# Expert stage of a fused mLSTM and two-layer MoE kernel: two output scalings of the first expert moved behind its third block, weight splits regrouped, one scaling of the last expert moved

## The chip, the cores and the metric

One NeuronCore of one Trainium2 chip runs the whole program in one launch. The metric is the device time of the program in microseconds (us), as a median of several executions. The engines are named as the profile names them: PE (TensorE), DVE (VectorE), ACT (ScalarE), POOL (GpSimd) and SP (SyncE, which here only issues DMAs).

## The reference, cut to what matters

Three layers follow one another. The change lies in the third alone.

```python
x = mlstm(q, k, v, gates)                 # (1536 tokens, 320)
x = leaky(x @ w_in) @ w_out               # dense layer, 320 -> 2048 -> 320
e = argmax(x @ w_gate, axis=1)            # each token goes to one of 8 experts
disp[e, slot] = x[token]                  # capacity 384 slots per expert
h = max(disp @ w1[e], 0)                  # 320 -> 1024
y = h @ w2[e]                             # 1024 -> 320
out[token] = gate_w[token] * y[e, slot]   # 0 where a token found no slot
```

## The kernel before, in words

**Layout of the expert stage** (lines 838 to 967). The routed rows lie in a DRAM buffer `scr`, 384 slots for each expert. An expert's slots are three blocks of 128, `j` = 0, 1, 2. For each block there are four steps:

- `hidden(e, j)` (L586 through `l1_chunk`): 8 chunks of 128 hidden units, each of 8 matmuls (values are kept as a high and a low float16 part), 64 matmuls in all, into two PSUM banks `h`, one for each half `u` of the chunks.
- `evict(e, j)`: for each half, ACT writes the high part `hh` with a ReLU (L888) and DVE the low part `hl` (L889).
- `outs(e, j)` (L590 to L592 through `l2_chunk`): 8 chunks of 3 matmuls, 24 in all, into the PSUM tile `py`. The first two of a chunk read `hh`, the third (L592) reads `hl`.
- `deliver(e, j)`: ACT scales `py` by the tokens' gate weight into `ye` (L900), and POOL issues an indirect DMA that scatters the rows of `ye` to the output (L901). The gate weights and token numbers come in one small load `mt` (L850).

**Blocks that are not there.** Block 0 is always computed. `if_block(e, j)` is a branch on PE alone: where expert `e` has no tokens in block `j`, PE jumps over `hidden` and `outs` of it. ACT and DVE still run their evictions and scalings for such a block. With these inputs 15 of the 24 blocks hold tokens: the experts 0 to 7 have 1, 2, 3, 2, 1, 1, 3 and 2 of them.

**Weights.** An expert's two matrices come in two pieces, so there are 16 pieces, 0 to 15; expert `e` uses 2e and 2e+1. A piece has an "in" part (from `w1`: a staging tile `wa`, loaded by L542 and L543) and an "out" part (from `w2`: a staging tile `wc`, loaded by L552). Each part must be split into a high and a low float16 half before PE may use it: ACT writes the high half (L498) and DVE the low half (L499). The in split is two instructions on each engine (128x1024 and 64x512), the out split one on each (128x1280). There are four staging tiles of each kind, and a load is issued when the split that last read its tile is done; SP issues loads in order.

**Order of the work.** The whole expert stage stands in `manual_schedule`: PE, ACT and DVE run their instructions in the order in which the code gives them. POOL's and SP's order is set by the framework's planner. The splits are laid in between the steps by hand: while expert `e` is computed, the pieces of `SPLITS[e]` are split, which are [4], [5, 6, 7], [8, 9, 10], [11, 12, 13], [14], [15], and none for the last two (L32). The list `bg` holds an in and an out split for each piece (and in expert 0 the out splits of the pieces 2 and 3 ahead of those of piece 4). `some(k)` (L926) runs the `k`-th quarter of `bg`, rounded down. The order within one expert on ACT and DVE is this: evict block 0, `some(0)`, deliver block 2 of the expert before, evict block 1, `some(1)`, deliver block 0, `some(2)`, deliver block 1, evict block 2, `some(3)`. PE's order is: hidden block 0, outs block 2 of the expert before, hidden block 1, outs block 0, outs block 1, hidden block 2. In the last expert there is no next one, so its blocks are closed on the spot (L958 to L967).

Of the kernel before, what the change touches and what calls it, by code (L numbers as in the profile page):

```python
# [75 lines left out]
def tile_mlstm_moe_moe(  # L76
# [191 lines left out]
    def run_all(fs):  # L268
        for f in fs:
            f()  # L270
# [259 lines left out]
    def w_place(n):  # L530
        staged[n, 2] = pool_of.get(n, wpb).tile([P, PCN], F16, tag="pc", name=f"pc{n}")
# [40 lines left out]
    def w_out_split(n):  # L572
        c = staged[n, 1]
        if n < NP1:
            rc, c = c, stage_out()
            narrow(c, rc)
        pieces[n][1] = piece_out(pieces[n][1], c, src_of(n)[3], n in PPOOL)
# [10 lines left out]
    def l2_chunk(py, n, kc, gh, gl, first, last):  # L588
        oh, ol = pieces[n][1]
        nc.tensor.matmul(py, lhsT=gh, rhs=oh[:, kc, :], start=first, stop=False)  # L590
        nc.tensor.matmul(py, lhsT=gh, rhs=ol[:, kc, :], start=False, stop=False)  # L591
        nc.tensor.matmul(py, lhsT=gl, rhs=oh[:, kc, :], start=False, stop=last)  # L592
# [87 lines left out]
    def apart(key, dma):  # L680

        tc.declare_no_dep(dma.ins, group=key, reason="each token has a row of its own")
        tc.add_to_no_dep_group(key, dma.ins)
# [139 lines left out]
    def w_load(n):  # L823
        w_alloc(n)
        w_load_in(n)
        w_load_out(n)
# [16 lines left out]
    def exp_load(e):  # L843
        X[e] = e2.tile([P, 6, NSLOT], F16, tag=f"xe{e % 2}", name=f"xe{e}")
        nc.sync.dma_start_transpose(out=X[e], in_=scr[e * NSLOT:(e + 1) * NSLOT, 0:384].bitcast(F16))

    def meta_load():

        mt = e2.tile([P, E, NJ, 2], F32, name="mt")
        nc.sync.dma_start(mt, scr[:, 384:386].rearrange("(e j p) c -> p e j c", p=P, j=NJ))  # L850
        ix = e2.tile([P, E, NJ], I32, name="ix")
        nc.gpsimd.tensor_scalar(out=ix, in0=mt[:, :, :, 0], scalar1=IDX0, scalar2=None, op0=ALU.add)
        T["meta"] = mt, ix
# [19 lines left out]
    def wn(e, c):  # L873
        return NP1 + e * NP2 + c // NKC, c % NKC
# [17 lines left out]
    def outs(e, j):  # L892
        hh, hl = hhl[e % 2]
        for c in range(NCK):
            l2_chunk(py[j], *wn(e, c), hh[:, c, j * P:(j + 1) * P], hl[:, c, j * P:(j + 1) * P], c == 0, c == NCK - 1)

    def deliver(e, j):
        mt, ix = (x[:, e] for x in T["meta"])
        ye = yes[e % 2]
        nc.scalar.activation(ye[:, j], py[j], AF.Copy, scale=mt[:, j, 1:2])  # L900
        apart("out", nc.gpsimd.indirect_dma_start(  # L901
            out=out, out_offset=bass.IndirectOffsetOnAxis(ix[:, j:j + 1], 0), in_=ye[:, j],
            in_offset=None, bounds_check=NT - 1, oob_is_err=False))
# [6 lines left out]
    for e in range(E):  # L910
        if e + 1 < E:
            exp_load(e + 1)
        if e == 0:
            meta_load()
        bg = [lambda: w_out_split(NP1 + 2), lambda: w_out_split(NP1 + 3)] if e == 0 else []
        for n in SPLITS[e]:
            n += NP1
            if (n, 0) not in staged:
                w_load(n)
            w_place(n)  # L920
            bg += [lambda n=n: w_in_split(n), lambda n=n: w_out_split(n)]
        for n in sum(SPLITS[e + 1:], [])[0:NLOAD]:
            if (NP1 + n, 0) not in staged:
                w_load(NP1 + n)

        def some(k, of=4):  # L926
            run_all(bg[k * len(bg) // of:(k + 1) * len(bg) // of])

        hidden(e, 0)
        if e == 0:  # L930
            for t in hs[NU:] + py[1:]:
                nc.vector.memset(t, 0.0)
        evict(e, 0)
        some(0)
        if e == 0:
            _, more = nc.values_load_multi_w_load_instructions(
                filled[0:1].rearrange("a e j -> a (e j)"), engines=[ENG.PE], min_val=0, max_val=1,
                skip_runtime_bounds_check_because="it is the outcome of a comparison")
        else:
            with if_block(e - 1, 2):  # L940
                outs(e - 1, 2)
            deliver(e - 1, 2)
        with if_block(e, 1):  # L943
            hidden(e, 1)
        evict(e, 1)
        some(1)
        outs(e, 0)
        deliver(e, 0)
        some(2)
        if e < E - 1:  # L950
            with if_block(e, 1):
                outs(e, 1)
                with if_block(e, 2):
                    hidden(e, 2)
            deliver(e, 1)
            evict(e, 2)
            some(3)
        else:  # L958
            with if_block(e, 2):
                hidden(e, 2)  # L960
            evict(e, 2)
            with if_block(e, 2):
                outs(e, 2)
            deliver(e, 2)
            with if_block(e, 1):
                outs(e, 1)
            deliver(e, 1)  # L967
    one.close()

# [28 lines left out]
```

## Time and profile before

| | us |
|---|---|
| median of three runs | 424.47 |
| the three runs | 424.04, 424.47, 424.86 |
| the profiled execution, whole | 424.7 |
| its span, first to last instruction | 423.0 |

The profiled execution is 0.23 us above the median of the runs, inside their spread of 0.82 us; its span leaves out 1.7 us that lie around it. All times of rows below count from the start of that span. The expert stage begins at 299.6 us and runs to the end, so it is 123 us of the 423.

How to read the rows: a row of a timeline gives start, length, engine, line, operation, what it writes and reads, and how many neighbouring instructions were merged; in square brackets stands how long the engine was idle just before, and what ended the idle time as the profile infers it. "PEq" is PE's sequencer (branches, semaphores), "PEld" its weight loads. The granted clock of PE is given as a share: 1.00 is 2.4 GHz, 0.50 is 1.2 GHz.

### The profile page before, as it was taken

The page shows a single profiled execution, that of the slowest core. Times are in us where ns is not written, and L with a number is a line of the kernel's source. Part 1 is how long each engine was busy: PE and PEld are TensorE (multiplying, and loading weights), DVE is VectorE, ACT ScalarE, POOL GpSimd, SP SyncE. Part 2 cuts the span into 40 slices and gives each one's busy share as a digit, 9 for nine tenths or more (in the row PEclk, how much of TensorE's full clock was granted, in tenths as well). Part 3 has the DMA queues.
Part 4 walks back from the last instruction along what each step waited for, and adds up shares of the span by engine and source line. Part 5 has one row for each costly group of instructions (what it writes and reads, how often), then busy time and mean ns, then how long its engine had stood idle before and what let it go on. Part 6 is the DMA issues. An engine that isn't in the chain of part 4 may idle for free. (4 is left out here: it accounts for less than half of the span.)

```text
span 423.0 us, 9186 instructions
## 1 busy us (share of the span) xinstructions
PE 367.9 (87%) x3597; PEld 286.3 (68%) x3597; DVE 300.8 (71%) x516; ACT 227.6 (54%) x440; POOL 170.8 (40%) x207
## 2 busy tenths in 40 slices
PE   0878657889799998999999999798779999789993
PEld 0767547668588875666656666595667898568882
DVE  8998999998669664877563374756689967866121
ACT  4461647427676747555355354751378966765222
POOL 4451651816446562465734373443124212222102
PEclk9999999669989999999999999999899999899999
DMA  9999999757998866099611349996197989722000
GB/s 172 218 296 233 262 246 211 126 108 154 210 191 122 176 153 135 2 240 180 152 43 32 60 158 302 303 238 195 45 218 218 312 223 347 169 63 61 33 17 19
DMA packets 146130, 70.22 MB, mean 166 GB/s; under 512 B 115666, under 2 KB 136692, under 8 KB 146080
## 3 DMA queue, kind: packets, MB, share of 16 engines
q1 hardware_dynamic: 144160, 65.44, 67.2%
q0 software_dynamic: 1920, 4.08, 2.7%
q8 instruction: 35, 0.57, 0.6%
q14 instruction: 15, 0.12, 0.1%
HBM read 43.65 MB, written 13.17 MB: 134 GB/s over the span
## 5 line engine op out<-in xcount | busy, mean ns | idle before, releaser
L586 PEld LDWEIGHTS <-pc 128*128 128x128 f16 x1728 | 117.9, 101 | 34.0 <-issue 11.5
L586 PE MATMUL h<-xT,pc 128*128 128x128 f16 (+3 forms) x768 | 99.6, 282 | 5.0 <-DMA xT<-xr 3.0
L801 POOL TENSOR_TENSOR gl<-t,gh 128x512 f16<-128x512 f32 (+1 forms) x52 | 60.0, 1155 | 63.6 <-ACT gh L800 63.4
L586 PE MATMUL h<-xe,pc 128*128 128x128 f16 x960 | 57.3, 222 | 5.5 <-PEq L940 2.0
L590 PE MATMUL px<-pc,gh 128*128 128x320 f16 x192 | 58.2, 305 | 2.1 <-ACT gh L800 2.1
L901 POOL DMA_INDIRECT out_dram<-ye,ix x24 | 26.7, 1114 | 81.1 <-ACT ye L900 80.1
L591 PE MATMUL px<-pc,gh 128*128 128x320 f16 x192 | 58.2, 305 | 0.0
L592 PE MATMUL px<-pc,gl 128*128 128x320 f16 x192 | 56.3, 306 | 0.6 <-POOL gl L801 0.6
L799 DVE SCALAR_TENSOR_TENSOR t<-h,t 128x512 f32<-128x512 f32 (+1 forms) x52 | 33.4, 644 | 30.0 <-ACT t L798 29.8
L889 DVE SCALAR_TENSOR_TENSOR hl<-h,hh 128x512 f16<-128x512 f32 x48 | 31.3, 685 | 32.4 <-ACT hh L888 32.3
L800 ACT ACTIVATE gh<-t 128x512 f16<-128x512 f32 (+1 forms) x52 | 30.9, 594 | 29.1 <-DVE t L799 28.6
L798 ACT ACTIVATE t<-h 128x512 f32<-128x512 f32 (+1 forms) x52 | 28.9, 555 | 29.5 <-PE h L586 28.9
L499 DVE SCALAR_TENSOR_TENSOR pc<-wa,pc 128x1024 f16<-128x1024 f32 (+1 forms) x36 | 36.9, 1024 | 8.9 <-ACT pc L498 6.8
L590 PE MATMUL py<-pc,hh 128*128 128x320 f16 x120 | 36.6, 305 | 3.1 <-PEq L943 2.3
L888 ACT ACTIVATE hh<-h 128x512 f16<-128x512 f32 x48 | 27.1, 594 | 21.5 <-PE h L586 20.2
L592 PE MATMUL py<-pc,hl 128*128 128x320 f16 x120 | 36.7, 306 | 1.6 <-DVE hl L889 1.5
L498 ACT ACTIVATE pc<-wa 128x1024 f16<-128x1024 f32 (+1 forms) x36 | 29.6, 863 | 15.3 <-DVE wa L483 9.0
L591 PE MATMUL py<-pc,hh 128*128 128x320 f16 x120 | 36.6, 305 | 0.0
L499 DVE SCALAR_TENSOR_TENSOR pc<-wc,pc 128x1280 f16<-128x1280 f32 x20 | 31.4, 1571 | 3.7 <-ACT pc L498 3.5
L498 ACT ACTIVATE pc<-wc 128x1280 f16<-128x1280 f32 x20 | 25.3, 1266 | 2.3 <-DVE wc L483 2.2
L590 PEld LDWEIGHTS <-gh 128*128 128x128 f16 x192 | 19.2, 100 | 10.8 <-ACT gh L800 2.6
L900 ACT ACTIVATE ye<-py,mt 128x320 f32<-128x320 f32 x24 | 12.4, 525 | 26.0 <-PE py L592 11.9
(178 smaller groups left out, 658.5 us busy)
## 6 DMA issues: line engine op xcount, KB each, us to landing
wc<-in_moe_w_dram SPq DMA_DIRECT2D x16, 640.0 KB, 6.5
wa<-in_moe_w_dram SPq DMA_DIRECT2D x16, 512.0 KB, 9.8
raw<-in_moe_w_out_dram SPq DMA_DIRECT2D x4, 1280.0 KB
scr<-zero SPq DMA_DIRECT2D x8, 588.0 KB, 4.4
raw<-in_moe_w_in_dram SPq DMA_DIRECT2D x4, 1024.0 KB
lb<-lam_d SPq DMA_DIRECT2D x8, 512.0 KB, 4.6
wa<-in_moe_w_dram SPq DMA_DIRECT2D x16, 128.0 KB
qkv<-in_k_dram SPq DMA_DIRECT2D x12, 160.0 KB, 2.9
```

The source lines that it names most:

```text
L498: nc.scalar.activation(hi, x, AF.Copy, scale=s)
L499: nc.vector.scalar_tensor_tensor(out=lo, in0=x, scalar=s, in1=hi, op0=ALU.mult, op1=ALU.subtract)
L586: nc.tensor.matmul(ph, lhsT=w, rhs=xT[:, x, 0:ncol], start=(m == 0), stop=(m == len(seq) - 1))
L590: nc.tensor.matmul(py, lhsT=gh, rhs=oh[:, kc, :], start=first, stop=False)
L591: nc.tensor.matmul(py, lhsT=gh, rhs=ol[:, kc, :], start=False, stop=False)
L592: nc.tensor.matmul(py, lhsT=gl, rhs=oh[:, kc, :], start=False, stop=last)
L798: nc.scalar.activation(t, ph, AF.Copy, scale=0.01 * S_G)
L799: nc.vector.scalar_tensor_tensor(out=t, in0=ph, scalar=S_G, in1=t, op0=ALU.mult, op1=ALU.max)
L800: mark[0] = nc.scalar.activation(gh, t, AF.Copy)
L801: nc.gpsimd.tensor_tensor(out=gl, in0=t, in1=gh, op=ALU.subtract)
L888: nc.scalar.activation(hh[:, to[0], to[1]], ph, AF.Relu)
L889: nc.vector.scalar_tensor_tensor(out=hl[:, to[0], to[1]], in0=ph, scalar=0.0, in1=hh[:, to[0], to[1]], op0=ALU.max, op1=ALU.subtract)
```

## The change

Three things, all in the loop over the experts, none of which touches what is computed.

1. `some(k)` rounds its bounds up where it rounded down. In expert 0 (four splits) nothing changes, one in each group. In experts 1 to 3 (six splits) the groups were 1, 2, 1, 2 and become 2, 1, 2, 1. In experts 4 and 5 (two splits) they were 0, 1, 0, 1 and become 1, 0, 1, 0.
2. In expert 0 the two `deliver` calls of the blocks 0 and 1 move behind the eviction of block 2 and the last group of splits.
3. In the last expert `deliver` of block 2 is given after `outs` of block 1, directly ahead of `deliver` of block 1.

```diff
         def some(k, of=4):
-            run_all(bg[k * len(bg) // of:(k + 1) * len(bg) // of])
+            run_all(bg[-(-k * len(bg) // of):-(-(k + 1) * len(bg) // of)])
...
         outs(e, 0)
-        deliver(e, 0)
+        if e > 0:
+            deliver(e, 0)
         some(2)
         if e < E - 1:
             with if_block(e, 1):
                 outs(e, 1)
                 with if_block(e, 2):
                     hidden(e, 2)
-            deliver(e, 1)
+            if e > 0:
+                deliver(e, 1)
             evict(e, 2)
             some(3)
+            if e == 0:
+
+                deliver(e, 0)
+                deliver(e, 1)
         else:
             with if_block(e, 2):
                 hidden(e, 2)
             evict(e, 2)
             with if_block(e, 2):
                 outs(e, 2)
-            deliver(e, 2)
             with if_block(e, 1):
                 outs(e, 1)
+            deliver(e, 2)
             deliver(e, 1)
```

## Rows read from the trace of the kernel before

**Rows 1.** Page, part 1: busy time of PE over the span.
```profile
PE 367.9 (87%) x3597; PEld 286.3 (68%) x3597; DVE 300.8 (71%) x516; ACT 227.6 (54%) x440; POOL 170.8 (40%) x207
```

**Rows 2.** Waits of PE, 299 to 423 us: total, times, longest.
```profile
PE py L592 <- DVE hl L889: 1.5, 1, 1.5
```

**Rows 3.** Timeline of PE in expert 4, `outs` of its only block.
```profile
365.78 0.30 PE L590 MATMUL py<-pc,hh 128*128 128x320 f16 x1 [0.57 <-PEq L943]
...
367.73 0.45 PE L592 MATMUL py<-pc,hl 128*128 128x320 f16 x1 [1.51 <-DVE hl L889]
...
371.16 0.30 PE L590 MATMUL py<-pc,hh 128*128 128x320 f16 x1
...
372.25 0.30 PE L592 MATMUL py<-pc,hl 128*128 128x320 f16 x1
```

**Rows 4.** Windows: length, busy (PE PEld DVE ACT POOL), PEclk, DMA share, GB/s.
```profile
365.78:367.73 1.95, 0.43 (x3) 0.11 (x3) 1.95 (x3) 1.95 (x5) 0.85 (x1) 1.00 0.98 303
367.73:371.14 3.41, 3.41 (x13) 1.94 (x14) 3.38 (x5) 1.30 (x2) 0.19 (x1) 0.50 0.05 12
371.14:372.60 1.46, 1.41 (x10) 0.78 (x8) 0.17 (x1) 0.00 (x0) 0.00 (x0) 1.00 0.00 0
```

**Rows 5.** Timeline of ACT, end of expert 3 and start of expert 4.
```profile
358.29 1.26 ACT L498 ACTIVATE pc<-wc 128x1280 f16<-128x1280 f32 x1
361.13 0.53 ACT L900 ACTIVATE ye<-py,mt 128x320 f32<-128x320 f32 x1 [1.57 <-issue]
361.55 1.07 ACT L888 ACTIVATE hh<-h 128x512 f16<-128x512 f32 x2
362.50 1.57 ACT L498 ACTIVATE pc<-wa 128x1024 f16<-128x1024 f32 x2
363.97 1.26 ACT L498 ACTIVATE pc<-wc 128x1280 f16<-128x1280 f32 x1
365.13 1.06 ACT L888 ACTIVATE hh<-h 128x512 f16<-128x512 f32 x2
```

**Rows 6.** Timeline of DVE in the same stretch.
```profile
359.72 1.49 DVE L499 SCALAR_TENSOR_TENSOR pc<-wc,pc 128x1280 f16<-128x1280 f32 x1
...
363.61 1.94 DVE L499 SCALAR_TENSOR_TENSOR pc<-wa,pc 128x1024 f16<-128x1024 f32 x2
365.58 1.49 DVE L499 SCALAR_TENSOR_TENSOR pc<-wc,pc 128x1280 f16<-128x1280 f32 x1
366.99 2.48 DVE L889 SCALAR_TENSOR_TENSOR hl<-h,hh 128x512 f16<-128x512 f32 x4
```

**Rows 7.** Timelines of ACT, DVE, PE and PEld, experts 0 and 1.
```profile
311.08 0.53 ACT L900 ACTIVATE ye<-py,mt 128x320 f32<-128x320 f32 x1 [2.29 <-DMA mt<-scr]
...
312.58 1.94 DVE L499 SCALAR_TENSOR_TENSOR pc<-wa,pc 128x1024 f16<-128x1024 f32 x2 [1.80 <-ACT pc L498]
314.56 1.29 DVE L889 SCALAR_TENSOR_TENSOR hl<-h,hh 128x512 f16<-128x512 f32 x2
...
315.51 3.58 PEld L586 LDWEIGHTS <-pc 128*128 128x128 f16 x64 [1.42 <-DVE hl L889]
315.52 3.74 PE L586 MATMUL h<-xe,pc 128*128 128x128 f16 x64 [1.25 <-PEq L940]
```

**Rows 8.** Timeline of PE's weight loads in expert 5, first `hl` of `outs`.
```profile
377.89 0.10 PEld L592 LDWEIGHTS <-hl 128*128 128x128 f16 x1 [0.39 <-DVE hl L889]
```

**Rows 9.** Line L951, PE's branch over an absent block 1: min/median/max ns, first, last.
```profile
L951 PEldq COMPARE_BRANCH  x7: 63/68/3846, 306.5 to 390.1; - x7
```

**Rows 10.** Timeline of POOL: two scatters one right behind the other.
```profile
374.72 0.98 POOL L901 DMA_INDIRECT out_dram<-ye,ix  x1 [0.30 <-ACT hh L888]
```

**Rows 11.** Timeline of SP, expert 3: load of piece 13, next `xe` load.
```profile
347.16 0.46 SPq L542 DMA_DIRECT2D wa<-in_moe_w_dram  x1
...
361.16 2.52 SPq L845 DMA_TRANSPOSE xe<-scr  x1
```

**Rows 12.** Line L542: time from issue of a `wa` load to its landing.
```profile
DMA to landing us min/median/max: 6.4/9.8/10.3
```

## The prediction

> **What bounds the kernel now.** I read the page first: PE is busy 87% of the span [rows 1], so a change in the expert stage is worth what it takes out of PE's own waits there. The second view was PE's waits from 299 us to the end. Most are branch costs of PE's sequencer, which no order on ACT or DVE touches. One is not: a single wait of 1.5 us for DVE's `hl` [rows 2]. The third view, PE's timeline, places it. In expert 4 `outs` starts at 365.78, and its third matmul, the first that reads `hl`, starts only at 367.73 [rows 3]. The fourth view, the windows, shows a second loss right behind. In the 3.41 us that follow, PE's granted clock is 0.50, the lower level of 1.2 GHz, in a stretch where PE never stops; in the 1.95 us before it PE was busy for 0.43 [rows 4].
>
> What both cost: the matmuls from 367.73 to 371.16 are 13 steps in 3.43 us, 0.264 each; those from 371.16 to 372.25 are 8 steps in 1.09 us, 0.136 each [rows 3]. Low clock: 13 x (0.264 - 0.136) = 1.66 us. Wait: without it the third matmul starts two steps after 365.78, at 366.05, so 1.68 us. The sum, 3.34 us, checks against the whole: `outs` of 24 matmuls lasts from 365.78 to 372.55, 6.77 us, where 23 steps of 0.136 and a last one of 0.30 make 3.43.
>
> Why DVE is late there: ACT and DVE run in order. ACT is released from the scaling of expert 3's block 1 at 361.13, evicts its absent block 2 (361.55), then splits both parts of piece 13 (362.50, 363.97), and only then evicts expert 4's block 0 (365.13) [rows 5]. DVE repeats that order: in split 363.61, out split 365.58, then `hl` of expert 4 from 366.99 [rows 6]; its first half ends about 367.7. In front of 361.13 ACT was idle for 1.57 us [rows 5]. That slot is what the regrouping can use.
>
> **The change part by part.**
>
> *Regrouping, experts 1 to 3.* The groups become 2, 1, 2, 1. In expert 3 the in split of piece 13 moves ahead of the scaling at 361.13, into the idle slot. On ACT the step from 362.50 to 363.97 shows that it takes 1.47 us; behind the out split of piece 12 (358.29, 1.16 to the next instruction by the step 363.97 to 365.13) it runs from 359.45 to 360.92, so the scaling still starts at 361.13 [rows 5]. ACT then evicts block 2 at 361.55 as now, the out split starts at 362.50 and expert 4's eviction at 363.66 instead of 365.13. DVE: the out split of piece 12 waits for ACT as now or a little less; I place it at 359.6, ending a step of 1.41 later (365.58 to 366.99) at 361.0. The in split follows for 1.97 (363.61 to 365.58) to 362.97, the two `hl` of block 2 for some 1.2 (half of the 2.48 for four) to 364.18, the out split to 365.59, and then the first `hl` of expert 4, 0.69 long, to 366.28 [rows 6]. PE wants it at 366.05, so 0.25 us of the wait is left. Ends: no wait is left, or all 1.51 (the rival "as before" below); I take 0.25 because every step of it is a row from the same stretch.
>
> With the wait down to 0.25 us PE has no stretch like the one that precedes the low clock [rows 4], so I let the 1.66 us go as well; that they stay is a rival. Gain: 3.34 - 0.25 = 3.09 us.
>
> By the Trainium skill, "TensorE: Matmul & The Clock Gate", section "Why this matters for your kernels", only a longer idle gap than this one of 1.51 us brings the clock down. By that rule the low stretch has another cause and stays, and only 1.43 us are gained; the trace, whose clock falls at the end of this wait, speaks against it.
>
> The other side of 2, 1, 2, 1: one more out split, 1.41 us of DVE [rows 6], now stands ahead of the eviction of block 1 in experts 1, 2 and 3. What waits behind it is `outs` of block 1. PE first runs `outs` of block 0, 24 x 0.136 = 3.3 us [rows 3], so this is covered wherever DVE is level with PE. It is least so in expert 1, where DVE works off what expert 0 left; there the second part helps, since DVE's idle 1.80 us at 312.58 [rows 7] exceeds the 1.41. If that cover were gone, PE would wait there for at most the 1.41 us. I cost it at nothing. Staging tiles come free no later than now, so no load on SP starts later, except that the planner may set SP's order anew (a rival).
>
> *Regrouping, experts 4 and 5.* The out split of piece 14 now stands ahead of the scaling of block 1 and the eviction of block 2, the in split ahead of the older scaling. The work in front of expert 5's eviction is the same. `outs` of expert 5 shows a small wait now: 0.39 us in the weight loads [rows 8], less one step of 0.136 about 0.25 on PE. DVE no longer waits for ACT in that stretch. Ends 0 and 0.25 gained; I take 0.15.
>
> *Expert 0.* ACT waits 2.29 us for `mt` in front of the scaling at 311.08, and DVE 1.80 in consequence [rows 7]. Behind it stand the split of piece 4, the eviction of block 2 and then expert 1's first eviction. After the change ACT does all of that meanwhile; the two scalings and their two scatters come when `mt` is there, with nothing behind them on POOL until the next scaling. The loads that wait for piece 4's staging tiles are issued up to 1.8 us sooner. Does PE gain? The profile says that the weight loads at 315.51 waited for `hl`, whose first half ends at 315.25, and that PE stood 1.25 us, ended by its sequencer at L940 [rows 7]. Taken at its word, about 0.9 us would go (1.25 less a branch cost of some 0.3). But the same hidden block comes right after the dearest branch of all, 3.85 us at L951 [rows 9], and PE's own stream may be what was late. The ends are 0.9 gained and, as the same bound the other way (weight loads now run beside that stream sooner), 0.9 lost. I take nothing, since PE's releaser is the sequencer and the `hl` row only coincides.
>
> By the Trainium skill, "Runtime: NRT & Kernel Launch", section "Instruction fetch mechanics", a taken branch out of the loaded pages waits for a fetch by DMA; the 3.85 us agree. That would put the 1.25 us on the fetch and give this part no gain, which is the 0 above; by the releaser alone the sum would be 0.9 lower.
>
> *Last expert.* ACT's order stays: scaling of block 2, then of block 1. If its wait is still for its own block, nothing changes. If it is now for the `outs` in front of it, both scalings come at the end, and the second scatter is issued one POOL step later, 0.98 + 0.30 = 1.28 us [rows 10]. Ends 0 and +1.28; I take 0.
>
> **Sum.** 3.09 + 0.15 = 3.24 us less. The profiled execution of 424.7 would become 421.5; its 0.23 us above the median are within the runs' spread, so from 424.47 I forecast **421.2 us**.
>
> **The rivals.**
>
> - *The low clock stays*: what is gained is the wait, 1.68 - 0.25 = 1.43, and 0.15, so 422.9 us. For it: the wait is short, and PE had a branch pause of 0.57 us in front of it as well, which stays [rows 3]. Against: the low stretch begins at 367.73, just where the wait ends [rows 3, 4].
> - *Expert 0 pays too*: 0.9 more, 420.3 us. For it: the releaser in the weight loads. Against: PE's own row names the sequencer.
> - *The last scaling waits for the last `outs`*: 421.2 + 1.28 = 422.5 us. The change in the last expert then does something; otherwise it does nothing.
> - *As before*: the wait in expert 4 keeps its 1.51 us, since DVE, not ACT, sets it and has as much to do; with the low clock behind it the time is 424.3 us. Against: between the end of its out split at 361.21 and the in split at 363.61 DVE has 2.40 us with only the 1.21 of two `hl` in it, so 1.2 us of idle time lie ahead of the critical `hl` and get filled [rows 6].
> - *Slower*: the in split of piece 13 now stands in front of the scaling at 361.13, so ACT stands if its load is not there. With a split start S, the first `hl` of expert 4 ends at S + 1.1 + 1.97 + 1.21 + 1.41 + 0.69 = S + 6.4, against 367.7 now: it decides from S = 361.3 on. The load is issued at 347.16 [rows 11] and the slowest of its line takes 10.3 us [rows 12], 357.5, so there is 3.8 us to spare. Only another order on SP undoes that: behind the next `xe` load (361.16 + 2.52) it would land at 374.0 and `hl` would end at 380.4, 12.7 us later than now, 437 us.
>
> **How the numbers follow.** Chances: forecast 0.66 (its own range 420.6 to 421.9), low clock stays 0.12, expert 0 pays too 0.08, last scaling waits 0.05, as before 0.04, slower 0.05. A measurement of this kernel can tell about 0.2%, 0.85 us, from no change. The first four are faster by more than that; since "as before" could fall either way and waits can turn up that no row shows, I put faster 0.88, same 0.06, slower 0.06. The range 420.1 to 423.0 holds the forecast, the rivals at 420.3, 422.5 and 422.9, and the 0.9 lost in expert 0; outside lie as before and slower, and the tails.
>
> **What would show each step.** Right: ACT's in split of piece 13 directly behind the out split of piece 12, no 1.57 us of idle time there; expert 4's eviction about 1.5 us sooner after the scaling; the wait of `outs` in expert 4 for `hl` at 0.3 us or less; PE's clock at 1.00 through experts 4 and 5; ACT without a wait for `mt` in front of piece 4. Wrong: a 0.50 stretch that remains, a new wait of `outs` on block 1 in expert 1, an ACT wait on a `wa` load, or the last two scatters back to back.

## The result and the profile after

The changed kernel takes 419.71 us (median of 7 runs, 418.33 to 420.72) where the kernel before, on the same chip, takes 424.04 (7 runs, 421.99 to 424.86): a ratio of 0.9907, 95% interval 0.988 to 0.9933. It is faster, as forecast, but by about 4 us and not 3.24: the time lies 0.4 us below the forecast range. The profiled execution of after took 420.25 us, its span is 418.5.

One profiled execution against one other says little about tenths of a microsecond here, so the comparison below uses several. Five profiles have the instruction order of before on PE, ACT, DVE and SP (before itself and the runs `last_only`, `control_look`, `scatter_late` and `gate_before`, told below), three that of after (after, `after_again`, `after_gate`). Each stretch runs from the start of PE's first matmul of a block to that of the next one named, read from PE's timeline.

| stretch of PE's timeline, us | before | order of before, mean of 5 | after | order of after, mean of 3 | difference of means | forecast |
|---|---|---|---|---|---|---|
| expert 0 to expert 1 | 10.95 | 10.55 | 10.28 | 10.66 | +0.11 | 0 |
| expert 1 to expert 4 | 50.93 | 51.48 | 50.00 | 50.02 | -1.46 | 0 |
| expert 4 to expert 5 | 11.23 | 10.58 | 8.42 | 8.22 | -2.36 | -3.09 |
| expert 5 to expert 6's third block | 23.07 | 23.02 | 22.37 | 22.70 | -0.32 | -0.15 |
| from there to PE's end | 21.57 | 21.57 | 21.57 | 21.57 | 0 | 0 |
| sum | 117.75 | 117.20 | 112.64 | 113.17 | -4.03 | -3.24 |

The -4.03 of the means agrees with the timed difference of 4.3. The part in expert 4 is a little smaller than forecast, and a part between experts 1 and 4 was forecast as nothing.

The page of after, part 1, shows PE's share of the span unchanged at 87%, and 5.6 us less of PE's busy time than in [rows 1] for the same 3597 matmuls. Of these, 3.1 us lie in the expert stage, where before has the lower clock at two places and after at none until its end; the other 2.5 us lie ahead of it, where the change touches nothing, and are a difference between two executions.

```profile
PE 362.3 (87%) x3597; PEld 283.1 (68%) x3597; DVE 296.2 (71%) x516; ACT 227.7 (54%) x440; POOL 177.0 (42%) x207
```

In PE's waits of after from 299 to 419 us (total, times, longest), the 1.5 us of [rows 2] are gone. What is left for `hl` is 0.56 us in the first `outs` of expert 0 and 0.17 in expert 5. The branch costs of PE's sequencer lead the list, as they did before:

```profile
PE py L590 <- PEq L943: 3.0, 3, 1.4
...
PE py L592 <- DVE hl L889: 0.7, 2, 0.6
```

PE's timeline of after in expert 4 answers to [rows 3]. The third matmul follows the second after 0.14 us, where it came 1.8 later before; the last of the 24 starts at 368.40:

```profile
365.28 0.30 PE L590 MATMUL py<-pc,hh 128*128 128x320 f16 x1 [1.01 <-PEq L943]
365.41 0.30 PE L591 MATMUL py<-pc,hh 128*128 128x320 f16 x1
365.55 0.30 PE L592 MATMUL py<-pc,hl 128*128 128x320 f16 x1
...
368.40 0.30 PE L592 MATMUL py<-pc,hl 128*128 128x320 f16 x1
```

The windows of after over the same 24 matmuls (length, busy PE, PEld, DVE, ACT, POOL, granted clock, DMA share, GB/s) show the upper clock throughout, against 0.50 in [rows 4]:

```profile
365.28:368.71 3.43, 3.42 (x24) 2.24 (x24) 3.37 (x6) 2.45 (x5) 0.98 (x1) 1.00 0.41 90
```

ACT's and DVE's timelines of after at the end of expert 3 answer to [rows 5, 6]. The in split of piece 13 (358.50) stands directly behind the out split of piece 12, the 1.57 us of idle time in front of the scaling (now at 360.18) are gone, and expert 4's first eviction starts 2.54 us after that scaling, before 4.00. DVE has the first `hl` of expert 4 done halfway through its 1.28 us from 364.62, before PE asks for it at 365.55:

```profile
357.34 1.26 ACT L498 ACTIVATE pc<-wc 128x1280 f16<-128x1280 f32 x1
358.50 1.56 ACT L498 ACTIVATE pc<-wa 128x1024 f16<-128x1024 f32 x2
360.18 0.53 ACT L900 ACTIVATE ye<-py,mt 128x320 f32<-128x320 f32 x1
360.60 1.07 ACT L888 ACTIVATE hh<-h 128x512 f16<-128x512 f32 x2
361.56 1.28 ACT L498 ACTIVATE pc<-wc 128x1280 f16<-128x1280 f32 x1
362.72 0.61 ACT L888 ACTIVATE hh<-h 128x512 f16<-128x512 f32 x1
...
360.05 1.93 DVE L499 SCALAR_TENSOR_TENSOR pc<-wa,pc 128x1024 f16<-128x1024 f32 x2
362.01 1.29 DVE L889 SCALAR_TENSOR_TENSOR hl<-h,hh 128x512 f16<-128x512 f32 x2
363.22 1.48 DVE L499 SCALAR_TENSOR_TENSOR pc<-wc,pc 128x1280 f16<-128x1280 f32 x1
364.62 1.28 DVE L889 SCALAR_TENSOR_TENSOR hl<-h,hh 128x512 f16<-128x512 f32 x2
```

ACT's and PE's timelines of after in experts 0 and 1 answer to [rows 7]. ACT splits piece 4 and evicts block 2 first, and still waits 1.26 us for `mt`, but now nothing that PE needs soon stands behind it. PE's pause between expert 1's two hidden blocks is 0.32 us, before 1.25:

```profile
307.89 1.57 ACT L498 ACTIVATE pc<-wa 128x1024 f16<-128x1024 f32 x2
309.82 1.08 ACT L888 ACTIVATE hh<-h 128x512 f16<-128x512 f32 x2 [0.36 <-PEq L952]
310.79 1.27 ACT L498 ACTIVATE pc<-wc 128x1280 f16<-128x1280 f32 x1
313.33 0.94 ACT L900 ACTIVATE ye<-py,mt 128x320 f32<-128x320 f32 x2 [1.26 <-DMA mt<-scr]
...
310.52 3.73 PE L586 MATMUL h<-xe,pc 128*128 128x128 f16 x64 [0.83 <-DMA xe<-scr]
314.57 1.62 PE L586 MATMUL h<-xe,pc 128*128 128x128 f16 x26 [0.32 <-PEq L940]
```

### The profile page after: what moved, and what is told of

Same layout as the page of the kernel before. It is cut to its first block, busy times and chain, and to the rows that moved or that the text cites. A ratio compares the mean times of both kernels' runs of the same rounds, so it can differ in the third digit from the quotient of the medians.

```text
span 418.5 us, 9184 instructions
## 1 busy us (share of the span) xinstructions
PE 362.3 (87%) x3597; PEld 283.1 (68%) x3597; DVE 296.2 (71%) x516; ACT 227.7 (54%) x440; POOL 177.0 (42%) x207
## 4 chain that ended last, share of the span: by engine, by line
PE 37%; issue 22%; POOL 12%; DMA 11%; DVE 10%; ACT 4%; SPq 2%; POOLq 1%; DVEq 0%; ACTq 0%
PE h L586 15%; POOL out_dram L901 6%; PE px L592 4%; PE px L590 4%; PE px L591 4%; DMA raw<-in_moe_w_in_dram 3%; POOL gl L801 3%; DMA lb<-lam_d 2%; DMA wc<-in_moe_w_dram 2%; PE pj L408 2%; PE pj L407 2%; ACT lb L321 1%; DVE pc L499 1%; PE pi L395 1%; DMA x2T<-x2r 1%
## 5 line engine op out<-in xcount | busy, mean ns | idle before, releaser
L801 POOL TENSOR_TENSOR gl<-t,gh 128x512 f16<-128x512 f32 (+1 forms) x52 | 65.3, 1257 | 63.2 <-ACT gh L800 63.0
L901 POOL DMA_INDIRECT out_dram<-ye,ix x24 | 30.0, 1251 | 71.0 <-ACT ye L900 70.4
L586 PE MATMUL h<-xe,pc 128*128 128x128 f16 x960 | 55.9, 219 | 3.6 <-PEq L940 1.0
L590 PE MATMUL py<-pc,hh 128*128 128x320 f16 x120 | 35.9, 299 | 3.8 <-PEq L943 3.0
L499 DVE SCALAR_TENSOR_TENSOR pc<-wc,pc 128x1280 f16<-128x1280 f32 x20 | 29.7, 1486 | 9.3 <-ACT pc L498 9.1
L591 PE MATMUL py<-pc,hh 128*128 128x320 f16 x120 | 35.9, 299 | 0.0
L592 PEld LDWEIGHTS <-gl 128*128 128x128 f16 x192 | 18.9, 99 | 13.1 <-POOL gl L801 5.7
```

What stands on the lines that cost most here:

```text
L499: nc.vector.scalar_tensor_tensor(out=lo, in0=x, scalar=s, in1=hi, op0=ALU.mult, op1=ALU.subtract)
L586: nc.tensor.matmul(ph, lhsT=w, rhs=xT[:, x, 0:ncol], start=(m == 0), stop=(m == len(seq) - 1))
L801: nc.gpsimd.tensor_tensor(out=gl, in0=t, in1=gh, op=ALU.subtract)
L901: apart("out", nc.gpsimd.indirect_dma_start(out=out, out_offset=bass.IndirectOffsetOnAxis(ix[:, j:j + 1], 0), in_=ye[:, j], in_offset=None ...
```

## The experiments

Ratios are to runs of the kernel before on the same chip in the same session, with 95% intervals. The letters in the first four quoted expectations belong to those texts; from the fifth run on, A is "ACT's wait for `mt` makes `hl` late, and PE waits", and C is "POOL's first scatter, issued just ahead of PE's branch L940, delays PE there".

### The three parts alone, and the wait filled

**The regrouping alone** (`regroup_only`):

```diff
-            run_all(bg[k * len(bg) // of:(k + 1) * len(bg) // of])
+            run_all(bg[-(-k * len(bg) // of):-(-(k + 1) * len(bg) // of)])
```

> The weight splits in groups of 2, 1, 2, 1 alone; expert 0 and the last expert as before. Theory A (the forecast's working): nearly all of the gain is here. The third matmul of outs in expert 4 waits 0.3 us or less where it waited 1.68, and the clock stays at 1.00 behind it: 3.1 to 3.3 us less than before, ratio about 0.9925. Theory B (expert 0's part pays as well, about 0.9 us in the first hidden block of expert 1): this part gives the same 3.1 to 3.3 us, and the hidden block of expert 1 still takes 4.7 us from start to release. Theory C (the two parts only pay together, since DVE's backlog of expert 0 now runs into outs of block 1 in expert 1): a new wait of about 0.2 to 1.4 us of PE for hl in expert 1, and a gain of 2 us or less.

Measured: 422.86 us, ratio 0.9944 (0.9917 to 0.997), some 2.4 us and not 3.1 to 3.3. In its profile expert 4's `outs` lasts 3.69 us, at the upper clock, with 0.27 us of the wait left, the size that the prediction put down.

**Expert 0's part alone** (`first_only`), all else as before:

```diff
-        deliver(e, 0)
+        if e > 0:
+            deliver(e, 0)
...
-            deliver(e, 1)
+            if e > 0:
+                deliver(e, 1)
             evict(e, 2)
             some(3)
+            if e == 0:
+                deliver(e, 0)
+                deliver(e, 1)
```

> Expert 0's two scalings behind its third block, nothing else. Theory A: ratio 1.000 within 0.2%; ACT no longer waits for mt ahead of piece 4, but the first hidden block of expert 1 ends when it did and the 1.68 us wait and the low clock in expert 4 stay. Theory B: about 0.95 us less, ratio about 0.9978, with the first hidden block of expert 1 taking 3.75 us instead of 4.7 from start to release, and all later steps shifted by the same amount.

Measured: 423.03 us, ratio 0.9942 (0.9913 to 0.997), again some 2.4 us, more than either theory expected. The part that was costed at nothing gives as much as the one that was costed at 3.24, within the intervals. In its profile expert 4 is as before (`outs` 6.79 us, low clock), and the stretch from expert 1 to expert 4 is 50.00 us, as in after.

**The last expert's part alone** (`last_only`):

```diff
-            deliver(e, 2)
             with if_block(e, 1):
                 outs(e, 1)
+            deliver(e, 2)
             deliver(e, 1)
```

> The last expert's scaling of block 2 given after outs of block 1, nothing else. All theories: ratio 1.000 within 0.2%, since ACT's order is the same; the scaling of block 2 still starts some 2.7 us before that of block 1. The rival of the forecast (the scaling waits for the last outs): both scalings back to back at the end, 1.28 us more, ratio 1.003. If the first hidden block of expert 1 takes 3.75 us here too, its 4.7 us of before are no property of the order but differ from one execution to the next.

Measured: 424.70 us, ratio 1.0001 (0.9968 to 1.0033). Every engine has the order of before, so this is also a second profile of before. It shows what the first one hid: here the stage starts at the upper clock, ACT reaches the scaling sooner and waits 5.43 us for `mt` instead of 2.29, and PE runs into two waits for `hl`. Its timelines of ACT, DVE and PE:

```profile
310.72 0.53 ACT L900 ACTIVATE ye<-py,mt 128x320 f32<-128x320 f32 x1 [5.43 <-DMA mt<-scr]
...
312.22 1.94 DVE L499 SCALAR_TENSOR_TENSOR pc<-wa,pc 128x1024 f16<-128x1024 f32 x2 [3.88 <-ACT pc L498]
...
311.80 1.95 PE L586 MATMUL h<-xe,pc 128*128 128x128 f16 x32 [0.32 <-PEq L940]
314.94 1.95 PE L586 MATMUL h<-xe,pc 128*128 128x128 f16 x32 [1.18 <-DVE hl L889]
...
317.54 0.31 PE L592 MATMUL py<-pc,hl 128*128 128x320 f16 x1 [0.38 <-DVE hl L889]
```

The second half of expert 1's second hidden block writes the PSUM bank that expert 0's absent block 2 held, so it waits until DVE has evicted that, and DVE stood 3.88 us behind ACT. The stretch from expert 1 to expert 4 takes 51.90 us here, 1.90 over the 50.00 of after.

**The wait in expert 4 filled** (`fill_e4`): 32 matmuls into a bank that is overwritten later, ahead of expert 4's `outs`, order otherwise as before.

```diff
+        if e == 4:
+            for c in range(UC):
+                l1_chunk(banks(e, 1)[0][:, c], *wn(e, c), X[e][:, :, P:2 * P], P)
         evict(e, 1)
         some(1)
```

> The kernel before with 32 matmuls more on PE, 1.79 us, in the wait of expert 4: half of the hidden layer of its second block, which has no tokens, so nothing that is delivered depends on it. ACT's and DVE's work and order are as before. If the wait is what brings the low clock: the matmuls fit into the 1.68 us, the clock stays at 1.00, outs of expert 4 ends about 1.5 us sooner, ratio about 0.9964. If the low stretch has another cause: it stays, and the time is that of before or 0.1 us more, ratio 1.000.

Measured: 425.00 us, ratio 0.9993 (0.9972 to 1.0014). In the profile the fill did what it should: `outs` starts 1.80 us later than in [rows 3] but then runs at the upper clock, as the windows of this run show (first the fill, then the 24 matmuls), and PE's last `outs` ends 1.22 us sooner than in before. In the time nothing of it can be told from no change, so neither expectation is met. More profiles (below) offer a reason: the low clock is not there in every execution. With it the fill saves 1.5 us, without it nothing; at the share found below that is an estimated 0.8 us in the mean, a ratio of 0.998, which lies inside the interval.

```profile
365.80:367.75 1.95, 1.95 (x34) 1.89 (x35) 1.95 (x3) 0.82 (x2) 0.85 (x1) 1.00 0.75 268
367.58:371.02 3.44, 3.42 (x27) 2.25 (x24) 3.17 (x5) 2.54 (x4) 0.36 (x1) 1.00 0.03 5
```

### What pays in expert 0, and where the regrouping pays

**ACT's wait for `mt` taken away** (`no_scale_e0`):

```diff
-        nc.scalar.activation(ye[:, j], py[j], AF.Copy, scale=mt[:, j, 1:2])
+        nc.scalar.activation(ye[:, j], py[j], AF.Copy, scale=mt[:, j, 1:2] if e > 0 else 0.5)
```

> The kernel before, order of work untouched; only expert 0's three output evictions multiply by the constant 0.5 instead of the gathered gate value, so ACT has no wait for mt there (the scaling of expert 0's outputs by their gate is left out; the scatter on POOL still waits for mt). Theory A, that expert 0's part pays because ACT no longer stands at mt: most of what expert 0's part gave alone, ratio 0.994 (0.991 to 0.997), expert 1's first hidden block at 3.75 us instead of 4.68 and no wait of PE for hl between 310 and 320. Rival, that it pays because some 1 us of ACT's work moved behind the third block's eviction: that work is still ahead here, ratio 0.998 to 1.000, the block still over 4.1 us.

Measured: 424.10 us, ratio 0.9976 (0.9942 to 1.001), between the two expectations. The profile holds a surprise: ACT no longer waits for `mt`, DVE is in time, and yet PE stands 1.66 us at L940, the same place and releaser as in before [rows 7]. Just ahead, POOL issues expert 0's first scatter (PE's and POOL's timelines):

```profile
312.03 3.73 PE L586 MATMUL h<-xe,pc 128*128 128x128 f16 x64 [1.30 <-PEq L951]
317.42 2.79 PE L586 MATMUL h<-xe,pc 128*128 128x128 f16 x47 [1.66 <-PEq L940]
...
313.97 1.24 POOL L901 DMA_INDIRECT out_dram<-ye,ix  x1 [0.28 <-ACT hh L888]
```

In the trace the branch itself stands at 314.62 on PE's sequencer, 0.65 us behind that issue. The same goes for the other profiles made by then: the pause at L940 was 1.24 to 1.66 us in the four in which the scatter was issued 0.65 to 0.85 us ahead of the branch (before, `regroup_only`, `fill_e4`, this one), and 0.32 us in the rest. From this came C.

**The regrouping in expert 3 alone** (`regroup_e3`):

```diff
-            run_all(bg[k * len(bg) // of:(k + 1) * len(bg) // of])
+            if e == 3:
+                run_all(bg[-(-k * len(bg) // of):-(-(k + 1) * len(bg) // of)])
+            else:
+                run_all(bg[k * len(bg) // of:(k + 1) * len(bg) // of])
```

> The kernel before with the grouping 2, 1, 2, 1 in expert 3 alone. If the whole gain of the regrouping is at expert 4's first output block, as the prediction's sum has it (3.09 us of its 3.24): ratio 0.9944 (0.992 to 0.997), that block at 3.4 to 3.7 us instead of 6.78 with no low clock in it, and the 0.4 us excess of expert 5's and 6's first hidden blocks stays. Rival, that the other experts' regrouping carries a good part: ratio 0.997 to 0.999.

Measured: 422.53 us, ratio 0.9962 (0.9937 to 0.9986). Expert 4's `outs` lasts 3.42 us at the upper clock. That is some 1.6 us of the 2.4 of the whole regrouping, with intervals that overlap: expert 4 carries most of it or all, and what the other experts add is too small for these runs.

**The changed kernel once more** (`after_again`), beside the parts:

> The changed kernel itself, beside the parts. If the two parts that gave something alone add up: 0.9944 x 0.9942 = 0.989, range 0.987 to 0.9925, the last output's later scaling giving nothing. If they share a gain (the low clock is only moved about): 0.992 to 0.995.

Measured: 420.39 us (6 runs) against 425.00, ratio 0.9885 (0.9841 to 0.9928). The parts add up: 0.9944 x 0.9942 = 0.9886.

**The load of `mt` cut in two** (`meta_split`), expert 0's 3 KB first:

```diff
-        nc.sync.dma_start(mt, scr[:, 384:386].rearrange("(e j p) c -> p e j c", p=P, j=NJ))
...
+        rows = scr[:, 384:386].rearrange("(e j p) c -> p e j c", p=P, j=NJ)
+        for at, n in ((0, 1), (1, E - 1)):
...
+            nc.sync.dma_start(mt, rows[:, at:at + n])
```

> The kernel before with the load of mt cut in two, expert 0's rows (3 KB) first, the other seven experts' (21 KB) behind it. If the load is slow because of its many small pieces, expert 0's part lands by 309, ACT waits under 0.5 us for it and the gain of expert 0's part appears without moving anything: ratio 0.994 to 0.997. If it is slow because it stands behind the transposed load of expert 1's inputs in the same queue, it lands at about 310 to 311 all the same: ratio 0.999 to 1.001.

Measured: 423.25 us, ratio 0.9955 (0.9923 to 0.9986). A gain as in the first expectation, but ACT still waits, 3.08 us. The small part is there at 312.05, 4.2 us after its issue began at 307.80, where the whole load took 6.5 us in `last_only` (304.22 to 310.72), whose stage starts at the upper clock as here. So the wait is 2.3 us shorter than the 5.43 there, by more than the 1.18 us that `hl` came late, and PE loses nothing to it (50.00 us from expert 1 to 4). That agrees with A, by one profile.

### The scatters held back

**First attempt** (`scatter_late`): expert 0's first two scatters given behind a one-column copy on POOL that reads `hl` of its third block.

```diff
         nc.scalar.activation(ye[:, j], py[j], AF.Copy, scale=mt[:, j, 1:2])
+        if (e, j) not in LATE:
+            scatter(e, j)
...
             evict(e, 2)
+            if e == 0:
+                scatter_behind(0, 2)
...
+    def scatter_behind(e, j):
+        nc.gpsimd.tensor_copy(gate, hhl[e % 2][1][:, 0, j * P:j * P + 1])
+        for at in sorted(LATE):
+            if LATE[at] == (e, j):
+                scatter(*at)
+
+    LATE = {(0, 0): (0, 2), (0, 1): (0, 2)}
```

> The kernel before; ACT's work and order untouched, only POOL's first two scatters of expert 0 wait, behind a one-column copy, for hl of expert 0's third block. Theory C, that PE's wait at the branch L940 behind expert 1's first hidden block comes from a scatter that POOL issues 0.65 to 1.2 us ahead of that branch (seen in the profiles of before, of the regrouping alone, of the constant scale and of the filled wait, 0.95 to 1.37 us each, and in none where the scatter comes later): PE's gap there is 0.5 us instead of 1.47, and the time falls by part of what expert 0's part gave, ratio 0.996 to 0.999; a wait of PE for hl, where ACT stands long at mt, stays. Theory A alone, that only ACT's wait for mt counts: the gap or a wait for hl of about 1 us stays, ratio 0.999 to 1.001.

Measured: 425.11 us, ratio 0.9989 (0.9956 to 1.0022). It tests nothing of C: POOL's order is the planner's, which put both scatters (313.58 and 314.95) ahead of the copy (316.51). With the order of before it is one more profile of it: ACT waits 5.36 us for `mt`, PE 1.17 and 0.39 for `hl`, and the pause at L940, with no scatter ahead of it, is 0.32.

**The same with the constant scale** (`no_scale_scatter`: this edit and that of `no_scale_e0`) and **on the changed kernel**, for the scatters ahead of experts 5 and 6 (`after_gate`):

```diff
+    LATE = {(4, 1): (5, 0), (5, 1): (6, 0)}
...
         evict(e, 0)
+        if e in (5, 6):
+            scatter_behind(e, 0)
```

> The kernel before with both: expert 0's outputs scaled by the constant 0.5 (their gate scaling is left out), so that ACT has no wait for mt, and its first two scatters behind hl of its third block. If expert 0's part pays by these two things, ACT's wait and the scatter at the branch: all of its gain without moving an instruction of ACT or DVE, ratio 0.994 (0.991 to 0.997), expert 1's first hidden block 3.75 us and no gap of PE over 0.6 us between its start and the start of expert 2 but those also there in the changed kernel. If the moved ACT work itself pays: 0.997 to 1.000.

> The changed kernel with the second scatter of experts 4 and 5 waiting for hl of the next expert's first block, so that none is issued some 1 us ahead of the branch L940 of experts 5 and 6. Theory C: expert 5's and 6's first hidden blocks last 3.75 us in every profile, where before and five of its variants show 4.1 to 4.3, and the time is up to 0.8 us under the changed kernel's: ratio to the kernel before 0.987 (0.984 to 0.991). If the 0.4 us have another cause, they are there in this profile too, or the ratio is 0.9885 to 0.991 as for the changed kernel.

Measured: 424.19 us, ratio 0.9969 (0.9935 to 1.0003), and 420.85 us, ratio 0.9903 (0.9872 to 0.9934). Here too the planner put the scatters first, so they are further profiles of the constant scale and of after. With the constant scale the scatter came 1.16 us behind the branch this time, and the stretch from expert 1 to 4 is 50.04 us. In `after_gate` the matmuls of the first hidden blocks of experts 5 and 6 take 3.73 us, but PE's pauses behind them are 1.05 and 0.71 us, in after 0.58 and 0.32: the 0.4 us are there, and nothing was learnt of their cause.

**The kernel before, one more profile** (`control_look`, no edit):

> The kernel before itself, one more profiled execution. Theory A and C together: expert 1's first two hidden blocks and what follows up to expert 2 cost 0.9 to 2.2 us more than in the changed kernel, as a gap at the branch L940 with a scatter 0.65 to 1.2 us ahead of it or as a wait for hl behind a wait of ACT for mt of over 3 us; the clock of expert 4's output block is low or not, its wait for hl of about 1.7 us is there in any case.

Measured: one run, 426.55 us, beside 425.25 for the median of before in that session. ACT waits 5.35 us for `mt`, the stretch from expert 1 to 4 is 50.79, and the pause at L940 is 0.32 us with the scatter 0.57 us behind the branch. Only 0.79 us are lost here, a little under the expected 0.9; PE was itself slowed: its clock was at the lower level from 308.51 on. Expert 4 shows the wait of 1.51 us and the low clock again (windows of this run):

```profile
369.95:373.30 3.35, 3.35 (x15) 1.87 (x14) 3.08 (x5) 0.83 (x2) 0.00 (x0) 0.50 0.04 6
```

**The scatters held back by their data** (`gate_no_scale`, `gate_before`): their indices are computed on POOL from `mt` and from zero times `hl` of the third block, so they can't be issued sooner.

```diff
+        nc.gpsimd.tensor_scalar(out=nought, in0=hhl[0][1][:, 0, 2 * P:2 * P + 2], scalar1=0.0, scalar2=None, op0=ALU.mult)
+        nc.gpsimd.tensor_tensor(out=sum_, in0=mt[:, 0, 0:2, 0], in1=nought, op=ALU.add)
+        nc.gpsimd.tensor_scalar(out=ixg, in0=sum_, scalar1=IDX0, scalar2=None, op0=ALU.add)
+        for j in range(2):
+            scatter(0, j, ixg[:, j:j + 1])
```

> The kernel before with expert 0's outputs scaled by the constant 0.5 (their gate scaling is left out) and its first two scatters held back by a true dependence: their indices are computed on POOL from mt and from hl of expert 0's third block. Theories A and C together: no wait of ACT for mt and no scatter ahead of the branch L940, so PE's gap there is 0.5 us, expert 1's first hidden block 3.75 us and the stretch from its start to the start of expert 4 50.0 us as in the changed kernel; ratio 0.994 to 0.997. Rival, that the stall at L940 has nothing to do with the scatter: it is there again, 1 us or more, in executions where the stage starts at the low clock; ratio 0.998.

Measured: 422.73 us, ratio 0.9974 (0.9946 to 1.0002). PE's timeline has no loss: expert 1's blocks start at 310.75 and 314.80, the stretch to expert 4 is 50.00 us. The stage starts at the upper clock in this profile and the next, so neither tests the rival that ties the pause at L940 to a start at the lower one.

> The kernel before with only the two scatters held back in the same way, ACT's wait for mt left in. Theory C: PE's gap at L940 is 0.5 us; what stays is A's, a wait for hl of 0.2 to 1.2 us in expert 1's second hidden block where ACT waits over 3 us for mt. The stretch from the start of expert 1 to that of expert 4 is 50.0 to 51.9 us; ratio 0.996 to 1.000. Rival: the gap at L940 of 1.4 us or more is there although no scatter is ahead of it.

Measured: 424.05 us, ratio 1.0021 (0.9989 to 1.0053), nothing gained. With no scatter anywhere near (the first at 320.48), the pause at L940 is 0.32 us, and A's loss is there in full, 51.92 us from expert 1 to 4 (timelines of ACT, PE and POOL; the branch is L955 in this kernel):

```profile
313.94 0.53 ACT L900 ACTIVATE ye<-py,mt 128x320 f32<-128x320 f32 x1 [5.35 <-DMA mt<-scr]
...
315.00 1.96 PE L586 MATMUL h<-xe,pc 128*128 128x128 f16 x32 [0.32 <-PEq L955]
318.17 1.95 PE L586 MATMUL h<-xe,pc 128*128 128x128 f16 x32 [1.21 <-DVE hl L889]
320.77 0.31 PE L592 MATMUL py<-pc,hl 128*128 128x320 f16 x1 [0.38 <-DVE hl L889]
...
320.48 1.07 POOL L905 DMA_INDIRECT out_dram<-ye,ixg  x1 [0.29 <-ACT pc L498]
```

**Two more profiles with the constant scale** (`no_scale_look`, `no_scale_look2`, the kernel of `no_scale_e0`):

> The kernel before with expert 0's outputs scaled by the constant 0.5 (their gate scaling is left out), one more profiled execution. Theory C: PE's gap at the branch L940 is over 1.4 us if POOL's first scatter of expert 0 is issued 0.65 to 1.2 us ahead of the branch, and 0.5 us if it comes later. Rival: the gap does not follow the scatter.

> The same once more: the gap at L940 is over 1.4 us with a scatter 0.65 to 1.2 us ahead of the branch and 0.5 us without, by theory C; it does not follow the scatter by the rival.

Measured: one run each, 422.03 and 422.92 us, beside 423.42 for before. The first started the stage at the lower clock like `no_scale_e0`, but its scatter is issued 0.53 us ahead of the branch (312.92 to 313.45), and the pause is 0.32 us (PE's and POOL's timelines). The second has the scatter 1.12 us behind the branch and 0.32 us, too. Both have no loss up to expert 4 (50.06 and 50.00).

```profile
314.92 3.74 PE L586 MATMUL h<-xe,pc 128*128 128x128 f16 x64 [0.32 <-PEq L940]
...
312.92 1.24 POOL L901 DMA_INDIRECT out_dram<-ye,ix  x1 [0.28 <-ACT hh L888]
```

### What they say together

Expert 0's part, by the stretch from expert 1 to expert 4 (50.00 us where nothing is lost):

| kernels | profiles | stretch, us |
|---|---|---|
| order of before, scaling by `mt` | 5 | 50.93, 51.90, 50.79, 51.88, 51.92 |
| the same with the regrouping or the fill | 3 | 51.11 (`regroup_only`), 51.72 (`regroup_e3`), 50.92 (`fill_e4`) |
| order of before, constant scale | 5 | 51.33, 50.06, 50.00, 50.04, 50.00 |
| `deliver` of expert 0 moved | 4 | 50.00, 50.00, 50.06, 50.00 |

A is shown where ACT stands long. In the five profiles in which it waits 4.49 to 5.43 us for `mt` (`last_only`, `control_look`, `scatter_late`, `gate_before`, `regroup_e3`) PE then waits for `hl`, and 0.8 to 1.9 us are lost; with the constant scale and no ACT or DVE instruction moved, none of five profiles has such a wait of PE. A is not the loss in every execution: in before, `regroup_only` and `fill_e4` ACT waits only 2.03 to 2.29 us, PE has no wait for `hl` in this stretch, and the 0.9 to 1.1 us lost are the pause at L940, which is also the loss of the one constant-scale profile with 51.33.

The timed gains of the three constant-scale kernels are 0.9969, 0.9974 and 0.9976, and each interval reaches past 1. Weighted by their intervals they give, as an estimate, 0.9973 (0.9955 to 0.9991), about half of what the move gave (0.9942). Whether the moved work itself pays for the rest is open.

C is only argued: four pauses of over 1.2 us at L940, each with a scatter issued 0.65 to 0.85 us ahead of the branch, and none in the other profiles, the nearest scatter of which came 0.53 us ahead. No run made such a collision on purpose. A rival stands beside it: all four are among the nine profiles whose stage starts at the lower clock (of the other five, two have the scatter 0.53 us ahead of the branch and 1.5 us behind it, and three have `deliver` moved).

Expert 4's low clock: of the 12 profiles in which PE waits for `hl` there, 7 show granted clock 0.50 behind the wait (`outs` 6.72 to 6.79 us) and 5 show 1.00 throughout (5.04 to 5.11). Of the 6 in which the wait is gone, nearly gone or filled, none shows it (3.42 to 3.69). What decides it in an execution that has the wait is not known. One of the 5, `scatter_late`, has the very wait of [rows 3] in PE's timeline:

```profile
367.46 0.31 PE L592 MATMUL py<-pc,hl 128*128 128x320 f16 x1 [1.51 <-DVE hl L889]
```

and the upper clock in the windows over the same `outs`:

```profile
365.51:370.64 5.13, 3.60 (x24) 2.18 (x24) 5.10 (x7) 3.26 (x6) 1.04 (x1) 1.00 0.36 116
```

## Why the prediction was right or wrong

**The step that failed** is expert 0's part: "I take nothing, since PE's releaser is the sequencer and the `hl` row only coincides." The runs show -1.46 us in the mean of the stage's profiles, and 0.9942, some 2.4 us, in time for this part alone. Its own upper bound, 0.9, was too low as well. The reading of the row was right for that one execution: PE's releaser there was the sequencer. The error was to take that execution for the kernel. It was one whose stage started at the lower clock (its first hidden block took 5.28 us, 3.85 in after), so ACT reached the scaling 9.2 us after the stage's first matmul, and `mt` was there 11.5 us after it: a wait of 2.29 us. In the four other profiles of the same order these are 7.8 and 13.1 to 13.2 us, the wait is 5.35 to 5.43, and PE then waits for `hl`: 1.17 to 1.21 and 0.38 to 0.39 us in three of them, 0.38 in `control_look`. So DVE's late `hl` is a bound that the profile of before doesn't show. The chain from ACT's wait over DVE's `hl` to PE, which the prediction wrote down and then set aside, is the mechanism that the runs show; how much of the timed gain it makes is open, as said above. The rival "expert 0 pays too" at 420.3, given 0.08, came nearest, in part by luck: the 0.9 us that it took were the pause at L940, not a wait for `hl`. And the errors of the sum partly cancel: this part was 1.46 us too small, the one in expert 4 0.7 too large.

**The regrouping** was right in its mechanism and in its first order of size. The in split went where it was put, expert 4's eviction came 1.46 us sooner after the scaling (forecast 1.5), and what is left of the wait is 0, 0.20 and 0.27 us in the three profiles of after's order, 0.27 in `regroup_only` (forecast 0.25; each is the length of `outs` less after's 3.42). The term for the clock, 1.66 us, was right in size, 1.67 between the means of the profiles with and without it (6.77 and 5.10), but it was counted as there in every execution. It is there in 7 of 12, which is 1.0 us in the mean. The -2.36 us in the table, against 3.09, are mainly this.

**The rival "the low clock stays"** falls: 0 of 6 profiles without the wait have it. With it falls, for this case, the rule of the Trainium skill that the prediction weighed ("TensorE: Matmul & The Clock Gate", section "Why this matters for your kernels"), that only a longer idle gap than this brings the clock down. The runs show the lower clock at this place behind a wait of 1.51 us and never without it, though not always with it.

**The rule on fetches** ("Runtime: NRT & Kernel Launch" of the Trainium skill, section "Instruction fetch mechanics") was used to support the 0. It says that a taken branch out of the loaded pages waits for a fetch. The trace shows PE standing 0.32 us behind L940 as a rule, and 1.24 to 1.66 us with a scatter just ahead; no run here shows the fetch itself. So it could be the cause of that pause, but it gave no reason for the 0: the pause is absent in four of five profiles of before's order, where this part pays by another way. It is absent in all four profiles with the scalings moved; that the move is the reason isn't shown.

**Experts 5 and 6**: 0.15 forecast, 0.32 in the means, with single profiles from 22.66 to 23.17 us before and 22.37 to 22.89 after. The 0.4 us at their first hidden blocks are something else: all four profiles of the last session (`gate_no_scale`, `gate_before` and the two behind them) show 22.66 with the grouping of before, the ten others with that grouping there 23.02 to 23.32. Whether they go with the session or its chip was not tested.

**The last expert**: nothing, as forecast. In after ACT's scalings there start 2.74 us apart (410.18 and 412.92), as in before (414.64 and 417.38), so the rival of the last scaling that waits falls.

**The slower rival** falls: no wait of ACT for a `wa` load appears where the split now stands (358.50, no idle time in front).

## What to carry to other kernels

An engine that runs in order and stands at a late load delays all that is queued behind it; whether the bound engine feels it depends on how early that engine comes, and another loss (here a low clock at the stage's start) can hide it in the one profile at hand. So when a row shows a wait of 2 us with work for the bound engine behind it, price it as if that engine came early, and take a second profile of the same kernel before costing it at nothing. A loss that comes in only part of the executions goes into the sum with its share.

## What the runs showed of the hardware that was not expected

- The same program has its stretches of low clock in different places. In the five profiles with before's order, the clock is at the lower level at the stage's start in one, at 308.51 in another and at neither place in three; the stage's first hidden block, 64 matmuls, takes 3.85 us at the upper level and 5.28 where the lower one covers most of it.
- PE's pause at one branch that it takes (L940 of expert 1), 0.32 us in fourteen profiles, was 1.24 to 1.66 us in the four in which POOL had issued an indirect DMA 0.65 to 0.85 us ahead of it.
- A load of 3 KB in pieces of 8 bytes was there 4.2 us after its issue began (`meta_split`), with a transposed load issued by SP right ahead of it; the whole table of 24 KB, in the same pieces and at the same place, took 4.8 us in before and 6.5 in the four other profiles of its order.
